# ReLU-squared attention and a PReLU feed-forward layer: quads 5 and 6 turned by transposing transfers, w_out's second half loaded later, FFN2's column halves reordered

## The chip, the cores and the metric

The kernel runs on one core of one Trainium2 chip. The metric is the time of one execution in microseconds (us), as the device reports it; lower is better. TensorE (PE) multiplies matrices, VectorE (DVE), ScalarE (ACT) and GpSimd (POOL) work on elements, SyncE (SP) only issues transfers. Sixteen DMA engines carry the transfers. Those that convert float32 to bfloat16 on the way are issued by POOL, the transposing ones and the stores of the output by SP.

## The reference

Attention with a squared ReLU in place of the softmax, then a feed-forward layer with a leaky ReLU of one slope for each hidden column:

```python
def _attn_ref(q, k, v):                     # (8, 12, 448, 64) each
    S = q.shape[2]
    scale = 1.0 / np.sqrt(q.shape[-1])
    scores = scale * np.matmul(q, k.transpose(0, 1, 3, 2))
    attn = np.maximum(scores, 0.0) ** 2 / S
    return np.matmul(attn, v).astype(np.float32)

def _moe_ref(x, w_in, w_out, alpha):        # w_in (768, 2048), w_out (2048, 768)
    h = x @ w_in
    g = np.maximum(h, 0.0) + alpha * np.minimum(h, 0.0)
    return (g @ w_out).astype(np.float32)
# x is the attention's output as (8 * 448, 768); the result is float32 (3584, 768)
```

## The kernel before

**Units.** Four heads of one batch are a quad; there are 24 quads, three to a batch, numbered through. The 448 positions of a head are split as 64 x 7, so that a quad's q or k is a tile raw of 128 x 2 x 7 x 64, and its v a tile vraw of the same shape. Scores, squares and attention go in seven chunks j to a quad.

**Stages of a quad.** `load_qk` (L97) and `load_v` (L104) bring the three tiles in, 224 KB each in bfloat16, issued by POOL. The matmuls of the scores need q and k with the head dimension on the partitions, tile T. There are two ways to make it. `turn_pe` transposes 28 blocks on TensorE against an identity (L152) into PSUM and copies them out (L155). `turn_dma` has DVE copy q and k into a tile perm (L160), and SP issues one transposing transfer perm to T (L162), 448 KB. Then for each chunk `score_mm` runs four matmuls (L174) into a pair of PSUM banks, `relu` empties the pair on ACT (L183) or DVE (L185, by the letter in a pattern such as "ADAAAAA"), and `square` multiplies the result with itself (L193 on DVE, L191 on ACT). Chunks whose square is still to be done wait in the list `late`; `sq(k)` does the next k. `attnv` runs 28 matmuls (L203) over the squares and v, and writes the quad's part of xT, one half by ACT (L213), one by DVE (L214).

**Feed-forward.** For each batch and each of 16 blocks ff of the hidden columns, `f1` runs six matmuls over xT and w_in (L237), two for each quad of the batch; `f1_out` applies the leaky ReLU with one instruction of ACT (L245) and one of DVE (L246), writes gT, and does one late square. `f2(sb, c, hf)` makes 128 rows (c of 7) and 384 columns (half hf of 2) of the output of two batches: 16 matmuls over gT and w_out (L260), a copy by ACT into one of four buffers osb (L262), two stores by SP (L268). Row chunks c = 0, 1, 2 of batches 0 and 1 need batch 0 alone.

**Order.** It is written out by hand; every engine works through its instructions in this order. PSUM has eight banks, and `take_bank`, `take_pair` and `hold` give out the one that was taken longest ago. Quads 0 to 5 are turned on TensorE, all later ones by transfers. After FFN1 of batch 0 come three groups of FFN2 in column half 0, for c = 0, 1 and 2, with the scores of quads 4 and 5 and attention of quads 3 and 4 between them. FFN1 of batch 1 begins with the matmuls of four blocks over quads 3 and 4, and attention of quad 5 among them. Then the other groups of FFN2 of batches 0 and 1 follow, with the scores of later quads between (`run`, `burst`). Batches 2 to 7 are one loop.

**Queues.** POOL issues all loads in the written order. Three raw buffers each for q and k mean that the load of quad n waits until quad n-3 has been turned. The weights w_out_sb lie in SBUF as two column halves of 1536 KB, one transfer each (L118); w_in_sb is 16 transfers. perm has two buffers, T four, vraw seven.

Of the kernel before, what the change touches and what calls it, by code (L numbers as in the profile page):

```python
# [11 lines left out]
BF16 = mybir.dt.bfloat16  # L12
# [8 lines left out]
def kernel(  # L21
# [10 lines left out]
    nc = tc.nc  # L32
    B, H, S, D = q.shape
# [25 lines left out]
    w_out_sb = singles.tile([128, 2, KF, HALF], BF16)  # L59
    alpha_sb = singles.tile([128, KF], F32)  # L60
    beta_sb = singles.tile([128, KF], F32)
    psum = ps_pool.tile([128, 8, 512], F32)


# [13 lines left out]
    def hold():  # L78

        i = min(range(8), key=lambda i: (taken[i], i))  # L80
        taken[i] = 10**9
        return i

    def take_bank():
        i = min(range(8), key=lambda i: (taken[i], i))
        take(i, 1)
        return psum[:, i]
# [4 lines left out]
    def load_qk(n):  # L92
        b, g = divmod(n, NG)
        for name, src in (("q", q), ("k", k)):
            t = raw_pool.tile([128, 2, NJ, D], BF16, tag=name, name=f"{name}raw")
            flat = src[b].rearrange("(m two) (pp j) d -> (two pp) m (j d)", two=2, j=NJ)
            nc.gpsimd.dma_start(out=t.rearrange("p m j d -> p m (j d)"), in_=flat[:, 2 * g:2 * g + 2])  # L97
            raw[(n, name)] = t

    def load_v(n):  # L100
        b, g = divmod(n, NG)
        t = v_pool.tile([128, 2, NJ, D], BF16, tag="v", name="vraw")
        flat = v[b].rearrange("(m two) (pp j) d -> (two pp) m (j d)", two=2, j=NJ)
        nc.gpsimd.dma_start(out=t.rearrange("p m j d -> p m (j d)"), in_=flat[:, 2 * g:2 * g + 2])  # L104
        vraw[n] = t
# [8 lines left out]
                nc.gpsimd.dma_start(out=w_in_sb[64 * hf:64 * hf + 64, :, e, lo:hi],  # L114
                                    in_=w_in_v[hf, e, :, :, lo:hi])

    def load_w_out(h):
        nc.gpsimd.dma_start(out=w_out_sb[:, h], in_=w_out_v[h])  # L118

    FIRST = 4  # L120
    first, flat0 = {}, {}
# [21 lines left out]
    T = {}  # L143

    def turn_pe(n, parts=(("q", 0, NJ, "D"), ("k", 0, NJ, "D"))):
        if n not in T:
            T[n] = T_pool.tile([128, 2, NJ, 128], BF16, tag="T", name="T")
        for name, lo, hi, eng in parts:
            ps = take_bank().bitcast(BF16)
            for j in range(lo, hi):  # L150
                for s in range(2):
                    nc.tensor.transpose(ps[64 * s:64 * s + 64, 128 * j:128 * j + 128], raw[(n, name)][:, s, j], ident)  # L152
            dst = T[n][:, "qk".index(name), lo:hi].rearrange("p j c -> p (j c)")
            copy = nc.vector.tensor_copy if eng == "D" else nc.scalar.copy
            copy(dst, ps[:, 128 * lo:128 * hi])  # L155

    def turn_dma(n):
        p = perm_pool.tile([128, 2, NJ, 2, D], BF16, tag="perm", name="perm")
        for i, name in enumerate("qk"):
            nc.vector.tensor_copy(p[:, i], raw.pop((n, name)).rearrange("p s j d -> p j s d"))  # L160
        t = T_pool.tile([128, 2, NJ, 128], BF16, tag="T", name="T")
        nc.sync.dma_start_transpose(out=t.rearrange("p a j c -> p (a j) c"),  # L162
                                    in_=p.rearrange("p a j s d -> p (a j s d)"))
        T[n] = t
# [31 lines left out]
    def attnv(n):  # L196
        ps = take_pair()
        vv = vraw.pop(n)
        for j in range(NJ):
            a = att.pop((n, j))  # L200
            for r in range(2):
                for s in range(2):
                    nc.tensor.matmul(ps[64 * s:64 * s + 64, r, :S],  # L203
                                     vv[64 * r:64 * r + 64, s, j, :],
                                     a[64 * r:64 * r + 64, s],
                                     start=(j == 0), stop=(j == NJ - 1))
        b, g = divmod(n, NG)
        if g == 0:
            xT[b] = xT_pool.tile([128, NG, 2, S], BF16, tag="xT", name="xT")
        if n == 0:  # L210
            nc.scalar.activation(xT[b][:, g], ps[:, :, :S], ACTF.Copy, scale=out_scale)
            return
        nc.scalar.activation(xT[b][:, g, 0], ps[:, 0, :S], ACTF.Copy, scale=out_scale)  # L213
        nc.vector.tensor_scalar(xT[b][:, g, 1], ps[:, 1, :S], out_scale, None, ALU.mult)  # L214
# [3 lines left out]
    def sc(chunks):  # L218

        for n, j, eng in chunks:  # L220
            late.append((n, j, relu(score_mm(n, j), eng)))

    def sq(k=99, eng="D"):
        for g in late[:k]:
            square(*g, eng)
        del late[:k]

    def run(chunks):
        sc(chunks)
        sq()  # L230
# [4 lines left out]
    def f1_mm(ps, b, ff, ks):  # L235
        for km in ks:
            nc.tensor.matmul(ps, w_in_sb[:, km // 2, km % 2, bass.ts(ff, 128)],  # L237
                             xT[b][:, km // 2, km % 2, :],
                             start=(km == 0), stop=(km == KM - 1))

    def f1_out(ps, b, ff):
        if b // 2 not in gT:
            gT[b // 2] = g_pool.tile([128, KF, 2 * S], BF16, tag="g", name="gT")
        neg = neg_pool.tile([128, S], F32, tag="neg", name="neg")
        nc.scalar.activation(neg, ps, ACTF.Relu, scale=-1.0)  # L245
        nc.vector.scalar_tensor_tensor(gT[b // 2][:, ff, (b % 2) * S:(b % 2) * S + S],  # L246
                                       neg, beta_sb[:, ff:ff + 1], ps, ALU.mult, ALU.add)
        sq(1)
# [6 lines left out]
    def f2(sb, c, hf, parts=((0, HALF),)):  # L255
        o = o_pool.tile([128, HALF], F32, tag="o", name="osb")
        for lo, hi in parts:
            ps = take_bank()[:, :hi - lo]
            for ff in range(KF):
                nc.tensor.matmul(ps, gT[sb][:, ff, bass.ts(c, 128)], w_out_sb[:, hf, ff, lo:hi],  # L260
                                 start=(ff == 0), stop=(ff == KF - 1))
            nc.scalar.copy(o[:, lo:hi], ps)  # L262
            for u in range(2):
                blk = 2 * c + u
                b, j = 2 * sb + blk // NJ, blk % NJ
                rows = out[b * S:(b + 1) * S].rearrange("(pp j) d -> j pp d", j=NJ)
                eng = nc.scalar if u and hi - lo < HALF else nc.sync
                eng.dma_start(out=rows[j][:, hf * HALF + lo:hf * HALF + hi], in_=o[64 * u:64 * u + 64, lo:hi])  # L268
# [4 lines left out]
    def ch(n, lo, hi, p=pat):  # L273
        return [(n, j, p[j]) for j in range(lo, hi)]
# [22 lines left out]
    sq(1)  # L297
    sc([(1, 4, "D"), (1, 5, "A"), (1, 6, "A")])
    sq(2)
    load_w_out(0)  # L300
    load_v(3)
    early = {}
    todo = []
# [8 lines left out]
    sc(ch(2, 0, 3, "AAA"))  # L312
    sq(3)
    attnv(1)
    load_qk(5)
    load_v(4)
    load_v(5)
    load_w_out(1)
    todo = [(ff, km) for ff in range(4) for km in range(4)]
    sc(ch(2, 3, 5, "AAAAAAA"))  # L320
    sq(2)
# [14 lines left out]
    def f1s(b, lo, hi):  # L336
        for ff in range(lo, hi):
            f1(b, ff)

    def load(n):  # L340
        if n < NQ:
            load_qk(n)
            load_v(n)
# [4 lines left out]
        load(n + 2)  # L348

    turn_pe(3)  # L350
    load_qk(6)
    load_v(6)
    f1s(0, 4, 6)
    sc(ch(3, 0, 3))
    f1s(0, 6, 8)
# [3 lines left out]
    f1_mm(ps, 0, 9, range(KM))  # L359
    turn_pe(4, (("q", 0, NJ, "A"), ("k", 0, NJ, "D")))  # L360
    f1_out(ps, 0, 9)
    load_qk(7)
    load_v(7)
    f1s(0, 10, 12)
    sc(ch(3, 6, 7) + ch(4, 0, 2, "AA"))
    f1s(0, 12, 16)
    f2(0, 0, 0)
    sc(ch(4, 2, 5, "AAADAAA"))
    attnv(3)
    sc(ch(4, 5, 7, "AAAAAAD"))  # L370
    turn_pe(5)
    sq(3)
    sq(2, "A")
    load_qk(8)
    load_v(8)
    f2(0, 1, 0)
    sc(ch(5, 0, 3))
    attnv(4)
    sc(ch(5, 3, 5, "AAAADAA"))
    sq(3)  # L380
    sq(2, "A")
    f2(0, 2, 0)
    sc(ch(5, 5, 7, "AAAAAAD"))
    sq(1, "A")
    sq(1)


    chunks = [(n, j) for n in range(2 * NG, NQ) for j in range(NJ)]
# [2 lines left out]
    def some(k):  # L391
        lo = at_c[0]
        at_c[0] = min(lo + k, len(chunks))
        return [(n, j, e) for (n, j), e in zip(chunks[lo:at_c[0]], "ADA")]

    def burst(n):

        sc(some(3))
        attnv(n)
        sc(some(2))  # L400
        sq()

    early = []
    for ff in range(4):
        ps = take_bank()[:, :S]
        f1_mm(ps, 1, ff, range(4))
        early.append(ps)
        if ff == 1:
            attnv(5)
    for ff in range(KF):  # L410
        if ff < 4:
            f1_mm(early[ff], 1, ff, range(4, KM))
            f1_out(early[ff], 1, ff)
        else:
            f1(1, ff)
        if ff in (1, 4, 7):
            turn_dma(6 + ff // 3)
        if ff == 11:
            load(9)
            load(10)  # L420
    f2(0, 3, 0)
    run(some(3))
    f2(0, 3, 1)
    f2(0, 0, 1)
    prepare(9)
    run(some(3))
    f2(0, 1, 1)
    run(some(3))
    f2(0, 2, 1)
    run(some(3))  # L430
    f2(0, 4, 0)
    burst(6)
    f2(0, 4, 1)
    f2(0, 5, 0)
    prepare(10)
    burst(7)
    f2(0, 5, 1)
    f2(0, 6, 0)
    burst(8)
    f2(0, 6, 1)  # L440

# [56 lines left out]
```

## Time and profile before

| what | us |
|---|---|
| median of 4 runs (388.07 to 388.64) | 388.3 |
| the profiled execution | 387.89 |
| its span, first to last instruction | 386.1 |
| TensorE busy: FFN1 matmuls L237 (768) | 149.8 |
| TensorE busy: FFN2 matmuls L260 (912) | 151.1 |
| TensorE busy: scores L174 (672) | 45.5 |
| TensorE busy: attention L203 (672) | 37.4 |
| DVE busy | 265.9 |
| ACT busy | 206.2 |
| transposing transfers L162 (18), issue to landing, shortest, median, longest | 3.4, 6.9, 13.1 |
| w_out's two halves, issue to landing | 14.5, 22.7 |

Each row of TensorE is the union of that group's instructions. A matmul's own duration is longer than its share, since matmuls are pipelined: one of 384 columns lasts 0.32 us, and 16 of them take 2.6 us together. "Issue to landing" of a transfer includes the time that it spends behind others. The 40 slices of the page are 9.65 us each; the digits are tenths. In the chain that ended last every piece starts when what released it was done, so that the difference between starts is what a piece costs on the way to the end.

### The profile page before, as it was taken

The numbers are of one execution on the slowest core, as the hardware profiler recorded it, in microseconds if no ns is written. First come the engines' busy times: TensorE is split into PE (matmuls) and PEld (weight loads), VectorE is DVE, ScalarE is ACT, GpSimd is POOL, SyncE is SP. The second block draws the span as 40 slices with busy tenths as digits, with TensorE's granted clock in tenths as the row PEclk, the third lists the DMA queues.
The fourth block names the chain that finished last, engine by engine and source line by source line (L and its number), as shares of the span: only waits on it lengthen the run. The fifth ranks groups of instructions, "written<-read, shape, count | busy, mean of one in ns | idle before, by whom it ended". The sixth has DMA issues, their size and how long they took to land.

```text
span 386.1 us, 7917 instructions
## 1 busy us (share of the span) xinstructions
PE 377.7 (98%) x3228; PEld 210.7 (55%) x3228; DVE 265.9 (69%) x421; ACT 206.2 (53%) x332; POOL 64.1 (17%) x95
## 2 busy tenths in 40 slices
PE   7799999999999999999999999999999999999996
PEld 5444564555665456555555455654555545655554
DVE  4987786776868978789655897689754887626300
ACT  5978696446454664465444654547543475434311
POOL 7557221421012202022100221020000000000000
PEclk9999999999999999999999999999999999999999
DMA  9999999999293765687192871936035300120023
GB/s 158 191 201 204 204 213 220 169 181 212 73 164 57 114 129 83 130 131 120 42 182 51 131 121 41 181 55 133 22 74 97 71 0 23 42 61 2 15 70 82
DMA packets 71365, 42.97 MB, mean 111 GB/s; under 512 B 38432, under 2 KB 71328, under 8 KB 71328
## 3 DMA queue, kind: packets, MB, share of 16 engines
q0 software_dynamic: 26768, 22.45, 40.1%
q1 hardware_dynamic: 44128, 19.65, 24.0%
q8 instruction: 25, 0.41, 0.4%
q10 hardware_dynamic: 432, 0.36, 0.3%
q14 instruction: 12, 0.10, 0.1%
HBM read 45.62 MB, written 11.01 MB: 147 GB/s over the span
## 4 chain that ended last, share of the span: by engine, by line
PE 94%; DVE 3%; DMA 1%; ACT 0%; ACTq 0%; issue 0%
PE psum L237 38%; PE psum L260 38%; PE psum L174 9%; PE psum L203 8%; DVE at L193 2%; DMA qfirst<-in_q_dram 1%; PE psum L152 1%; DVE T L155 1%; DVE rl L185 1%; ACT osb L262 0%; ACTq L268 0%; ACT T L155 0%; DVE qraw L136 0%; ACTq L262 0%
## 5 line engine op out<-in xcount | busy, mean ns | idle before, releaser
L260 PE MATMUL psum<-w_out_sb,gT 128*128 128x384 bf16 (+2 forms) x912 | 151.1, 323 | 0.0
L237 PE MATMUL psum<-xT,w_in_sb 128*128 128x448 bf16 x768 | 149.8, 353 | 0.0
L260 PEld LDWEIGHTS <-gT 128*128 128x128 bf16 x912 | 86.7, 98 | 63.0 <-issue 8.2
L237 PEld LDWEIGHTS <-w_in_sb 128*128 128x128 bf16 x768 | 73.6, 98 | 72.3 <-issue 5.7
L246 DVE SCALAR_TENSOR_TENSOR gT<-neg,beta_sb,psum 128x448 bf16<-128x448 f32 x128 | 83.2, 677 | 29.8 <-ACT neg L245 29.8
L245 ACT ACTIVATE neg<-psum 128x448 f32<-128x448 f32 x128 | 69.2, 546 | 63.3 <-PE psum L237 59.6
L183 ACT ACTIVATE rl<-psum 128x896 bf16<-128x896 f32 x112 | 97.3, 935 | 0.5 <-PE psum L174 0.5
L193 DVE TENSOR_TENSOR at<-rl 128x896 bf16<-128x896 bf16 x162 | 90.7, 618 | 0.0
L185 DVE TENSOR_SCALAR rl<-psum 128x896 bf16<-128x896 f32 x56 | 60.8, 1087 | 43.1 <-PE psum L174 43.1
L262 ACT COPY osb<-psum 128x384 f32<-128x384 f32 (+2 forms) x57 | 27.0, 473 | 105.3 <-PE psum L260 98.5
L174 PE MATMUL psum<-T 64*64 64x448 bf16 x672 | 45.5, 356 | 2.8 <-DVE T L155 1.0
L97 POOL DMA_DIRECT2D qraw<-in_q_dram x23 | 16.6, 720 | 168.7 <-DVE perm L160 161.0
L203 PE MATMUL psum<-at,vraw 64*64 64x448 bf16 x672 | 37.4, 351 | 0.3 <-DVE at L193 0.2
L203 PEld LDWEIGHTS <-vraw 64*64 64x64 bf16 x672 | 24.1, 106 | 10.8 <-issue 2.9
L174 PEld LDWEIGHTS <-T 64*64 64x64 bf16 x672 | 18.2, 105 | 21.4 <-issue 14.4
L214 DVE TENSOR_SCALAR xT<-psum 128x448 bf16<-128x448 f32 x23 | 14.4, 625 | 16.3 <-PE psum L203 11.9
L97 POOL DMA_DIRECT2D kraw<-in_k_dram x23 | 16.6, 722 | 15.7 <-DMA w_out_sb<-in_moe_w_out_dram 14.2
L104 POOL DMA_DIRECT2D vraw<-in_v_dram x24 | 17.5, 729 | 1.8 <-DMA qraw<-in_q_dram 0.7
L213 ACT ACTIVATE xT<-psum 128x448 bf16<-128x448 f32 x23 | 12.6, 550 | 3.3 <-PE psum L203 3.3
L160 DVE COPY perm<-qraw 128x896 bf16<-128x896 bf16 x18 | 11.0, 613 | 2.5 <-DMA T<-perm 2.5
L114 POOL DMA_DIRECT2D w_in_sb<-in_moe_w_in_dram x16 | 10.1, 630 | 7.4 <-DMA kraw<-in_k_dram 2.3
L160 DVE COPY perm<-kraw 128x896 bf16<-128x896 bf16 x18 | 11.0, 609 | 0.0
(24 smaller groups left out, 40.8 us busy)
## 6 DMA issues: line engine op xcount, KB each, us to landing
out_dram<-osb SPq DMA_DIRECT2D x110, 96.0 KB, 2.2
vraw<-in_v_dram POOLq DMA_DIRECT2D x24, 224.0 KB, 7.9
qraw<-in_q_dram POOLq DMA_DIRECT2D x23, 224.0 KB, 4.9
kraw<-in_k_dram POOLq DMA_DIRECT2D x23, 224.0 KB, 6.7
w_in_sb<-in_moe_w_in_dram POOLq DMA_DIRECT2D x16, 192.0 KB, 8.4
w_out_sb<-in_moe_w_out_dram POOLq DMA_DIRECT2D x2, 1536.0 KB, 18.6
qfirst<-in_q_dram SPq DMA_DIRECT2D x1, 448.0 KB, 4.2
T<-perm SPq DMA_TRANSPOSE x18, 6.9
```

The source lines that it names most:

```text
L97: nc.gpsimd.dma_start(out=t.rearrange("p m j d -> p m (j d)"), in_=flat[:, 2 * g:2 * g + 2])
L160: nc.vector.tensor_copy(p[:, i], raw.pop((n, name)).rearrange("p s j d -> p j s d"))
L174: nc.tensor.matmul(ps[64 * c:64 * c + 64, r, :S], t[64 * r:64 * r + 64, 1, j, 64 * c:64 * c + 64], t[64 * r:64 * r + 64, 0, :, 64 * c:64 * ...
L183: nc.scalar.activation(rl, ps[:, :, :S], ACTF.Relu)
L185: nc.vector.tensor_scalar(rl, ps[:, :, :S], 0.0, None, ALU.max)
L193: nc.vector.tensor_tensor(a, rl, rl, ALU.mult)
L203: nc.tensor.matmul(ps[64 * s:64 * s + 64, r, :S], vv[64 * r:64 * r + 64, s, j, :], a[64 * r:64 * r + 64, s], start=(j == 0), stop=(j == NJ ...
L237: nc.tensor.matmul(ps, w_in_sb[:, km // 2, km % 2, bass.ts(ff, 128)], xT[b][:, km // 2, km % 2, :], start=(km == 0), stop=(km == KM - 1))
L245: nc.scalar.activation(neg, ps, ACTF.Relu, scale=-1.0)
L246: nc.vector.scalar_tensor_tensor(gT[b // 2][:, ff, (b % 2) * S:(b % 2) * S + S], neg, beta_sb[:, ff:ff + 1], ps, ALU.mult, ALU.add)
L260: nc.tensor.matmul(ps, gT[sb][:, ff, bass.ts(c, 128)], w_out_sb[:, hf, ff, lo:hi], start=(ff == 0), stop=(ff == KF - 1))
L262: nc.scalar.copy(o[:, lo:hi], ps)
```

## The change

Quad 5 is turned by a transposing transfer in place of TensorE, right after FFN1 of batch 0, and quad 6 after the scores of quad 4 in place of FFN1 of batch 1. The loads of q and k of quad 5 are issued ahead of w_out's first half, which comes in four transfers of four blocks ff each. GpSimd copies one element of quad 5's T into a new tile `landed` between the loads of quad 6's q and k and those of quads 7 and 8, and w_out's second half, also in four transfers, is issued behind the loads of quads 9 and 10 during FFN1 of batch 1. The square of chunk (4, 1) is kept back behind quad 5's turn. Groups 1 and 2 of FFN2 now lie next to each other; the scores of quad 5 follow them, the last two chunks among the early FFN1 matmuls of batch 1, which now are five blocks in held banks. FFN2 does all groups of column half 0 before those of half 1.

```diff
--- before.py
+++ after.py
@@ -59,6 +59,7 @@
     w_out_sb = singles.tile([128, 2, KF, HALF], BF16)
     alpha_sb = singles.tile([128, KF], F32)
     beta_sb = singles.tile([128, KF], F32)
+    landed = singles.tile([1, 1], BF16)
     psum = ps_pool.tile([128, 8, 512], F32)
 
 
@@ -114,8 +115,9 @@
                 nc.gpsimd.dma_start(out=w_in_sb[64 * hf:64 * hf + 64, :, e, lo:hi],
                                     in_=w_in_v[hf, e, :, :, lo:hi])
 
-    def load_w_out(h):
-        nc.gpsimd.dma_start(out=w_out_sb[:, h], in_=w_out_v[h])
+    def load_w_out(h, step=KF):
+        for lo in range(0, KF, step):
+            nc.gpsimd.dma_start(out=w_out_sb[:, h, lo:lo + step], in_=w_out_v[h][:, lo:lo + step])
 
     FIRST = 4
     first, flat0 = {}, {}
@@ -297,7 +299,8 @@
     sq(1)
     sc([(1, 4, "D"), (1, 5, "A"), (1, 6, "A")])
     sq(2)
-    load_w_out(0)
+    load_qk(5)
+    load_w_out(0, 4)
     load_v(3)
     early = {}
     todo = []
@@ -312,10 +315,8 @@
     sc(ch(2, 0, 3, "AAA"))
     sq(3)
     attnv(1)
-    load_qk(5)
     load_v(4)
     load_v(5)
-    load_w_out(1)
     todo = [(ff, km) for ff in range(4) for km in range(4)]
     sc(ch(2, 3, 5, "AAAAAAA"))
     sq(2)
@@ -348,8 +349,6 @@
         load(n + 2)
 
     turn_pe(3)
-    load_qk(6)
-    load_v(6)
     f1s(0, 4, 6)
     sc(ch(3, 0, 3))
     f1s(0, 6, 8)
@@ -359,30 +358,37 @@
     f1_mm(ps, 0, 9, range(KM))
     turn_pe(4, (("q", 0, NJ, "A"), ("k", 0, NJ, "D")))
     f1_out(ps, 0, 9)
-    load_qk(7)
-    load_v(7)
     f1s(0, 10, 12)
     sc(ch(3, 6, 7) + ch(4, 0, 2, "AA"))
-    f1s(0, 12, 16)
+    f1s(0, 12, 14)
+    kept = late[:]
+    del late[:]
+    f1s(0, 14, 16)
+    turn_dma(5)
+    late += kept
+    load_qk(6)
+    nc.gpsimd.tensor_copy(landed, T[5][:1, 0, 0, :1])
+    load_qk(7)
+    load_qk(8)
+    load_v(6)
+    load_v(7)
+    load_v(8)
     f2(0, 0, 0)
+    sq()
     sc(ch(4, 2, 5, "AAADAAA"))
     attnv(3)
     sc(ch(4, 5, 7, "AAAAAAD"))
-    turn_pe(5)
     sq(3)
     sq(2, "A")
-    load_qk(8)
-    load_v(8)
+    sq()
+    turn_dma(6)
     f2(0, 1, 0)
+    f2(0, 2, 0)
     sc(ch(5, 0, 3))
+    sq(1)
     attnv(4)
     sc(ch(5, 3, 5, "AAAADAA"))
-    sq(3)
-    sq(2, "A")
-    f2(0, 2, 0)
-    sc(ch(5, 5, 7, "AAAAAAD"))
-    sq(1, "A")
-    sq(1)
+    sq()
 
 
     chunks = [(n, j) for n in range(2 * NG, NQ) for j in range(NJ)]
@@ -401,41 +407,46 @@
         sq()
 
     early = []
-    for ff in range(4):
-        ps = take_bank()[:, :S]
-        f1_mm(ps, 1, ff, range(4))
-        early.append(ps)
+    for ff in range(5):
+        early.append(hold())
+        f1_mm(psum[:, early[ff], :S], 1, ff, range(4))
         if ff == 1:
+            sc(ch(5, 5, 7))
+            sq(1)
+            sq(1, "A")
+        if ff == 3:
             attnv(5)
     for ff in range(KF):
-        if ff < 4:
-            f1_mm(early[ff], 1, ff, range(4, KM))
-            f1_out(early[ff], 1, ff)
+        if ff < 5:
+            f1_mm(psum[:, early[ff], :S], 1, ff, range(4, KM))
+            f1_out(psum[:, early[ff], :S], 1, ff)
+            take(early[ff], 1)
         else:
             f1(1, ff)
-        if ff in (1, 4, 7):
-            turn_dma(6 + ff // 3)
-        if ff == 11:
+        if ff in (1, 4):
+            turn_dma(7 + ff // 3)
+        if ff == 6:
             load(9)
             load(10)
+            load_w_out(1, 4)
     f2(0, 3, 0)
     run(some(3))
-    f2(0, 3, 1)
-    f2(0, 0, 1)
+    f2(0, 4, 0)
+    f2(0, 5, 0)
     prepare(9)
     run(some(3))
+    f2(0, 6, 0)
+    run(some(3))
+    f2(0, 0, 1)
+    run(some(3))
     f2(0, 1, 1)
-    run(some(3))
+    burst(6)
     f2(0, 2, 1)
-    run(some(3))
-    f2(0, 4, 0)
-    burst(6)
-    f2(0, 4, 1)
-    f2(0, 5, 0)
+    f2(0, 3, 1)
     prepare(10)
     burst(7)
+    f2(0, 4, 1)
     f2(0, 5, 1)
-    f2(0, 6, 0)
     burst(8)
     f2(0, 6, 1)
```

## The prediction

> Times are us from the start of the profiled span. "T5" is quad 5's tile T, q5, k5, v5 its three loads, f2(c,h) FFN2's group of row chunk c and column half h of batches 0 and 1.
>
> **What bounds the kernel.** I read the busy table and the 40 slices first, then the waits of TensorE, then the chain that ended last in order of time from 44 on, then the transfers with their landings.
>
> ```profile
> PE 377.7 (98%) x3228; PEld 210.7 (55%) x3228; DVE 265.9 (69%) x421; ACT 206.2 (53%) x332; POOL 64.1 (17%) x95
> ...
> PEclk9999999999999999999999999999999999999999
> DMA  9999999999293765687192871936035300120023
> ```
>
> TensorE is the bound, at an undiminished clock. Its waits add up to 4.8 and all lie before 20. The DMA engines are full for ten slices, to about 96, and nearly idle late: what the change moves among the transfers lies in the full part, where a late transfer can take the place of the work removed. The chain there is TensorE without a hole, columns start, duration, work:
>
> ```profile
> 45.27 2.60 PE psum L260 x16
> 47.87 0.69 PE psum L174 x12
> 48.56 1.39 PE psum L203 x28
> 49.95 0.38 PE psum L174 x8
> 50.33 0.90 PE psum L152 x28
> 51.24 2.71 PE psum L260 x16
> 53.94 0.69 PE psum L174 x12
> 54.63 1.39 PE psum L203 x28
> 56.03 0.38 PE psum L174 x8
> 56.41 2.71 PE psum L260 x16
> 59.11 0.50 PE psum L174 x8
> 59.61 1.62 PE psum L237 x8
> 61.23 1.45 PE psum L203 x28
> 62.68 16.75 PE psum L237 x88
> ```
>
> The reader is to see the 0.90 at 50.33: quad 5's 28 transposes, the only work that the change takes from TensorE. Quad 6 is turned by a transfer already. The row of those transfers, then POOL waiting for a landing:
>
> ```profile
> T<-perm SPq DMA_TRANSPOSE x18, 6.9
> ...
> DMA to landing us min/median/max: 3.4/6.9/13.1
> ```
>
> ```profile
> 44.93 0.71 POOL L97 DMA_DIRECT2D kraw<-in_k_dram  x1 [7.01 <-DMA w_out_sb<-in_moe_w_out_dram]
> ```
>
> **TensorE's new order, summed.** From 45.27 with the durations above: f2(0,0) 2.60; 12 score matmuls 0.69; attnv(3) 1.39; 8 score matmuls 0.38; f2(1,0) 2.71 and f2(2,0) 2.60 (a group after another FFN2 group costs 2.60: two together are 5.31 in the chain at 82.73), to 55.64; 12 scores 0.69; attnv(4) 1.39; 8 scores 0.38; 8 early FFN1 matmuls 1.62; 8 scores 0.50; 8 early 1.62; attnv(5) 1.45, to 63.29; then the other 80 FFN1 matmuls. These last: 16.75 less eight at 0.19 (96 take 18.16 late in the chain, 8 take 1.62, so 0.188 each and 0.12 for a block's start), 15.25, to 78.54. Before it was 79.44. Saved: **0.90**. Two block starts decide its bounds: joining f2(1,0) to f2(2,0) saves 0.11, splitting the early FFN1 matmuls once more costs 0.12. Without the one 0.78, without the other 1.01. After 78.54 the columns change their order only; the sequence of FFN2 groups, score runs and bursts has the same lengths, so nothing is added.
>
> **DVE and ACT.** Two copies out of PSUM (0.62 each) go, two perm copies (0.61 each) come: even. The stretch from 55.64 to 63.29 now has no FFN2 group between quad 5's scores. By the spacing of consecutive rows (ACT: relu 0.80, square 0.87, xT 0.44, osb 0.37; DVE: relu 1.00, square 0.54, xT 0.54) ACT has 5.7 of work in these 7.65 and DVE 5.8. The tightest points: the square of chunk 6 on ACT ends at about 62.6, attnv(5) reads it at 61.84 + 6/7 x 1.45 = 63.08; the second half of xT leaves DVE at 64.07 (0.15 after attnv's end as at 62.83, then 0.63) and FFN1 reads it four early matmuls and one more later, at 64.35. PSUM banks, followed through the rotation, are free at each step. I cost this at nothing; the cover is 0.3 to 0.5. The 1-element GpSimd copy costs DVE nothing that a row shows; it blocks POOL's queue, see below.
>
> **q5 and k5 ahead of w_out's first half.** Loads land in order. k4 landed at 36.7 (issued 29.16, 7.5 to landing), the first half at 44.4 (29.88 + 14.5): 7.7 for 1536 KB. Five 224 KB loads then took 44.4 to 50.05, 1.13 each. Now q5 and k5 go first, to 38.95, and the quarters land at 40.9, 42.8, 44.7 and 46.65. f2(0,0) reads the last quarter after 12 of 16 matmuls, at 47.22: margin 0.57, cost nothing. From above: the second half took 8.5 (50.05 to 58.56, beside output stores); at that pace the last quarter lands at 47.45 and costs 0.24. A gain is excluded: f2(0,0) waits for nothing now. v3 lands at 47.8 for attnv(3) at 48.56. v4 and v5 keep their 50.05, since the same set lies before them.
>
> **T5.** On DVE the gT rows of ff 14 and 15 start at 45.66 and 46.79 with a square of 0.54 between; the change holds that square back, so ff 15 starts at 46.25, the perm copies at 46.84 and 47.38, done at 47.99. SP issued the first transfer 0.08 after its copies (67.62 to 67.70), so 48.07. POOL's queue has v4 to k6 in flight, as k8, v8 and the next loads were at 67.70; that transfer took 6.9. T5 lands at 54.94, scores need it at **55.64**: no stall, margin 0.70. From both sides: alone it was 3.4; the longest with no transposing transfer ahead were 8.06 (issued at 107.78 and 150.84, behind two output stores on the same queue), which here means 56.13 and a stall of 0.5. I take 6.9, the row with the same company. The stores of f2(0,0) stand behind T5 on SP; four osb buffers cover them, and without that cover only ACT's copy of a later group waits.
> The Trainium skill (VectorE: DVE Perf Modes, The three transpose paths and Rules for kernel authors) speaks against this step: transpose 128x128 on TensorE if a PSUM destination will do, with 390 ns there against 1309 ns by DMA. By it quad 5's 14 blocks would take an estimated 18.3 by DMA, T5 would land at 66.4, and the kernel would lose about 9.9. The trace does not bear out that price: all 14 blocks of a quad landed in 3.4 to 13.1.
>
> **q6 and k6, T6.** Without T5 k6 would land at 50.05 + 2 x 1.13 = 52.3. Beside a transfer the second load landed together with it (132.56: T at 139.35, k at 139.30; 165.57: 172.45 and 172.48), so k6 at about 55. DVE reaches T6's copies at 53.2, waits there, and is done at 55.6; queued behind is the relu of (5,1), ready at 56.1, and behind it the pair of banks that chunk (5,4) takes at 57.9. Some 0.5 are spare; if T5 is late, this is late with it. T6 itself is first read at 81.1 and would land at 62.8.
>
> **w_out's second half.** POOL now waits for T5 (about 55) before q7 to v8 (seven loads, 0.72 each to issue); q9, k9, v9 follow; q10 waits until T7's copies free its buffer (about 67.5); then come k10, v10 and the quarters. First need: f2(0,1) at 78.54 + 2.60 + 0.69 + 5.31 + 0.69 + 2.71 + 0.69 = 91.23, its last quarter at 93.3. Landing: q7 at 55.1 + 4.4 (3.9 and 4.8 from the rows at 105.58 and 67.40) = 59.5; 12 loads 13.6; the half 7.7; then T6, T7, T8. What a transfer takes from the loads: from 69.70 to 95.35 twelve loads landed, 13.6 of 25.65; six stores of 96 KB at 200 GB/s are 2.9; T6 to T8 and most of a fourth transfer share the other 9.1, 2.4 each, or 4.0 if the stores and the fourth cost nothing. So 59.5 + 13.6 + 7.7 + 7.2 + 2.0 (four stores) = 90.0, or 92.8 with 4.0 and no stores. With 8.5 for the half and T9 (issued at about 88) beside its end, 95. I take 90, cost nothing. The loads behind it, 11 and 12, are due only in batch 2.
> The skill (Advanced Engine Details and Errata, X-Bar Transpose) has transposing transfers as fast as regular ones, 350 to 400 GB/s; T's 448 KB would then be an estimated 1.2 each and the half would land some 3.6 earlier. No such transfer landed within less than 3.4 here.
>
> **Sum.** The profiled execution took 387.89 (span 386.1, 1.8 around it). Less 0.90: 386.99, span 385.2. The median of the runs is 388.3, 0.41 above that execution: 387.4.
>
> **Rivals.**
> (a) *T5 or k6 late.* The wait moves to the scores of quad 5, or to DVE at T6's copies. For: margin 0.7 and 0.5, rows of 8.06. Against: those rows had stores ahead. Price 0.2 to 0.7: 387.9.
> (b) *f2(0,0) waits for the last quarter*, or attnv(3) for v3. For: margin 0.57 on an estimated landing. Against: the pace of 1.13 and 7.7 is steady up to 50. Price 0.2 to 0.6: 387.8.
> (c) *Slower: w_out's second half late at f2(0,1).* Place: its last quarter at 93.3. For: every load from q7 on stands behind T5, the engines are full to 96 already, and three transfers lie among them. Against: loads 11 and 12 no longer precede it, about 6.8 of the 95.35. At a landing of 93.3 it begins to cost, at 94.2 the gain is gone, from 95.0 it is slower by over 0.2%. With 95.3 the wait is 2.0: 389.4.
> That the transposes stay in another form can be excluded: only L152 makes them.
>
> **How the numbers follow.** 0.2% is 0.78, about what a measurement tells from no change; my forecast of 0.90 lies just beyond. Forecast 0.52 (faster 0.44, same 0.08, as its own range is 387.1 to 387.6); (a) 0.16 (0.04, 0.09, slower 0.03); (b) 0.10 (0.02, 0.07, 0.01); (c) 0.22 (0, 0.04, 0.18). Together faster 0.50, same 0.28, slower 0.22. The range goes from 386.9 (saving 1.01 and scatter of the runs) to 389.4 ((c)'s price).
>
> **What would show it.** Right: L152 with 140 matmuls; T5 landing before 55.6; no wait of TensorE after 45; FFN1 of batch 1 ending about 0.9 earlier than 79.4. Wrong: a wait of L174 on T's transfer or on DVE near 56, of L260 on w_out near 47 or near 91 to 95; or a DVE row at L160 held beyond 56.

## The result and the profile after

The changed kernel takes 387.67 us (median of 42 runs, 387.17 to 388.36), the kernel before 388.26 (60 runs): a ratio of 0.9985, 95% interval 0.9981 to 0.9989. That is 0.59 us less, or 0.15%, with an interval that leaves out no change; it is two thirds of the 0.90 that was forecast, and below the 0.78 (0.2%) that the prediction took for what a measurement just tells from no change. The stated range of 386.9 to 389.4 holds the time.

The busy table and the slices of the changed kernel:

```profile
PE 377.7 (98%) x3200; PEld 211.1 (55%) x3200; DVE 266.3 (69%) x422; ACT 205.4 (53%) x331; POOL 67.8 (18%) x102
...
PEclk9999999999999999999999999999999999999999
DMA  9999999999993666598292772946036300120023
```

TensorE has 28 instructions less, the clock is whole, and the DMA engines are now full for twelve slices in place of ten. The chain that ended last, in order of time, over the stretch that the prediction summed:

```profile
45.86 2.60 PE psum L262 x16
48.46 0.69 PE psum L176 x12
49.15 1.39 PE psum L205 x28
50.55 0.38 PE psum L176 x8
50.93 5.31 PE psum L262 x32
56.23 0.69 PE psum L176 x12
56.92 1.39 PE psum L205 x28
58.31 0.38 PE psum L176 x8
58.69 1.62 PE psum L239 x8
60.31 0.50 PE psum L176 x8
60.81 1.62 PE psum L239 x8
62.43 1.45 PE psum L205 x28
63.88 15.24 PE psum L239 x80
```

The row of the transposes is gone, two FFN2 groups are one piece of 5.31, and no wait has come in. FFN1 of batch 1 ends at 79.12; from the first FFN2 group that is 33.26, where it was 34.17: 0.91 saved. But everything here is 0.59 later than forecast, and the span is 386.0 against 386.1. Two other stretches must have given the gain back. The first is the start. The first FFN1 matmuls in the chain, before and after:

```profile
20.21 0.91 PE psum L237 x4
```

```profile
20.80 0.92 PE psum L239 x4
```

The difference is made between 5 and 8 us, around quad 0's turn. The second is the end. ACT's last two copies of output, timeline of ACT, kernel before and then the changed one (start, duration, and in brackets the idle time before):

```profile
381.72 0.37 ACT L262 COPY osb<-psum 128x256 f32<-128x256 f32 x1 [1.27 <-PE psum L260]
...
382.72 0.27 ACT L262 COPY osb<-psum 128x128 f32<-128x128 f32 x1 [0.62 <-PE psum L260]
```

```profile
381.69 0.37 ACT L264 COPY osb<-psum 128x256 f32<-128x256 f32 x1 [1.55 <-PE psum L262]
...
382.68 0.27 ACT L264 COPY osb<-psum 128x128 f32<-128x128 f32 x1 [0.63 <-PE psum L262]
```

The changed kernel's last matmul starts at 382.00, before it was 382.32, 0.32 earlier; the copy starts only 0.03 to 0.04 earlier. Measured from the start of the last matmul of its own group (381.37 and 381.05), the first of the two copies starts after 0.35 before and after 0.63 in the changed kernel; the second waits for ACT's own store in between and is late with it. The chain has the same place as follows, before and then in the changed kernel. ACTq is the end of ACT's wait for TensorE, and "issue" is time in which ACT waited for nothing that the profile shows:

```profile
381.66 0.03 ACTq L262
381.68 0.04 issue
381.72 0.38 ACT osb L262
```

```profile
381.34 0.03 ACTq L264
381.37 0.32 issue
381.69 0.38 ACT osb L264
```

ACT had TensorE's signal 0.32 earlier and began only 0.04 earlier: 0.28 is lost at the very end, behind TensorE.

### The profile page after: what moved, and what is told of

The parts are those of the page before. It is cut to its first block, busy times and chain, and to the rows that moved or that the text cites. A ratio compares the mean times of both kernels' runs of the same rounds, so it can differ in the third digit from the quotient of the medians.

```text
span 386.0 us, 7874 instructions
## 1 busy us (share of the span) xinstructions
PE 377.7 (98%) x3200; PEld 211.1 (55%) x3200; DVE 266.3 (69%) x422; ACT 205.4 (53%) x331; POOL 67.8 (18%) x102
## 4 chain that ended last, share of the span: by engine, by line
PE 94%; DVE 3%; DMA 1%; issue 0%; ACT 0%; ACTq 0%
PE psum L239 38%; PE psum L262 38%; PE psum L176 9%; PE psum L205 8%; DVE at L195 2%; DMA qfirst<-in_q_dram 1%; PE psum L154 1%; DVE T L157 1%; DVE rl L187 1%; ACT osb L264 0%; ACTq L270 0%; DVE qraw L138 0%; ACTq L264 0%
## 5 line engine op out<-in xcount | busy, mean ns | idle before, releaser
L195 DVE TENSOR_TENSOR at<-rl 128x896 bf16<-128x896 bf16 x164 | 91.8, 618 | 0.0
L187 DVE TENSOR_SCALAR rl<-psum 128x896 bf16<-128x896 f32 x55 | 59.8, 1086 | 43.6 <-PE psum L176 43.6
```

Source lines behind the costliest of these rows:

```text
L187: nc.vector.tensor_scalar(rl, ps[:, :, :S], 0.0, None, ALU.max)
L195: nc.vector.tensor_tensor(a, rl, rl, ALU.mult)
```

## The experiments

### Where the missing 0.3 is: the start

The new tile `landed` is allocated in SBUF ahead of the first loads' tiles and moves all that follow. Three kernels ask whether that costs the 0.3: the changed one with the tile behind all others, the kernel before with an unused tile, and the changed one with quad 5 turned on TensorE again.

```diff
 # landed_last: a pool of its own behind the others
-    landed = singles.tile([1, 1], BF16)
+    landed = landed_pool.tile([1, 1], BF16)
 # landed_only: the kernel before
+    landed = singles.tile([1, 1], BF16)
```

> The changed kernel with the tile landed taken from a pool behind all others, so that no other tile moves in SBUF (in the changed kernel landed takes 32 bytes ahead of the first tiles, raw and all that follow). Theory S, the moved addresses cost about 0.3 us in the first 12 us: 387.35 us, first FFN1 matmul at about 20.2 as before. Theory N, the 0.3 that are missing from the predicted 0.90 are lost elsewhere: 387.67 us as the changed kernel, first FFN1 matmul anywhere from 20.2 to 20.8.

> The kernel before with the tile landed allocated at the changed kernel's place and never used, so that the same tiles move by 32 bytes and nothing else changes. Theory S: 388.55 us, 0.3 slower than before, first FFN1 matmul at about 20.8. Theory N: 388.26 us, no difference.

landed_last: 387.39 us (11 runs), ratio 0.9978, 0.9970 to 0.9987; first FFN1 matmul at 20.32. landed_only: 388.23, ratio 1.0004, 0.9996 to 1.0013; first FFN1 matmul at 20.51. Neither time alone tells S from N. The first interval holds 387.35 and 387.67, and the second holds no change and the 0.3 of S (1.0008); but landed_only's fastest run, 387.85, is that of the kernel before beside it, 387.86, where S wants 0.3 more. The profiles decide: two kernels below that keep the moved tiles (pe5, act_minus1) start FFN1 at 20.21, as the kernel before, and act_minus1 profiled a second time starts it at 20.59. So theory S falls. The start differs from one execution to the next (20.2 to 20.8 over the profiles) and goes with none of the edits; what makes it differ is open.

```diff
 # pe5: the changed kernel
-    turn_dma(5)
     late += kept
-    nc.gpsimd.tensor_copy(landed, T[5][:1, 0, 0, :1])
     sc(ch(4, 5, 7, "AAAAAAD"))
+    turn_pe(5)
     sq(3)
```

> The changed kernel with quad 5 turned on TensorE again, where it was turned before, and without GpSimd's copy; the tile landed keeps its place, everything else stays moved. Both theories: 0.90 us more than the changed kernel, 388.55 us, 28 transposes of 0.90 in the chain. If the other moves hide a gain or a loss of their own, it is not 0.90: 388.26 would say that they cost 0.3.

pe5: 388.24 us, ratio 1.0005, 0.9996 to 1.0014. By the medians that is 0.57 more than the changed kernel, not 0.90. The chain of pe5 says 0.90 all the same:

```profile
45.27 2.60 PE psum L262 x16
...
50.33 0.90 PE psum L154 x28
51.23 5.31 PE psum L262 x32
...
79.43 2.60 PE psum L262 x16
```

From 45.27 to 79.43 is 34.16, the kernel before to 0.01. From there to the start of TensorE's last matmul it is 302.88 in pe5, in the kernel before and in the changed one. So the moved loads, the other order of the column halves and the merged groups together neither gain nor lose anything on TensorE; the whole gain is the 28 transposes. In pe5 the first of the last two copies starts 0.65 after its last matmul, like in the changed kernel: the late end came with the edits around, not with the turn. Its fastest run, 388.10, is 0.93 above the changed kernel's 387.17; the ratios are 0.20% or 0.78 us apart, and their intervals are too wide to tell 0.57 from 0.90.

### Where the missing 0.3 is: the end

Counted over all of ACT's records in the trace, semaphore waits included, the late copy is number 576 in every kernel in which it is late, and 575 in those in which it is not (the expectations count one more). The change made the program one longer, 584 records in place of 583; the page shows one less (331 against 332), since it leaves the waits for semaphores out. Two kernels move the copy by one, by giving the square of chunk (5, 6) to the other engine.

```diff
 # act_minus1: the changed kernel
-            sq(1)
-            sq(1, "A")
+            sq(2)
 # before_act_plus1: the kernel before
-    sq(1, "A")
-    sq(1)
+    sq(2, "A")
```

> The changed kernel with the square of chunk (5, 6) on DVE in place of ACT, so that ACT's program has one instruction less and the first of the last two osb copies is its 576th and not its 577th. Theory T, that instruction begins 0.28 us late because of its position in ACT's program: the copy follows the last matmul's start by 0.35 us as before, and the time is 387.4 us. Rival R, the late copy belongs to the moved loads or to the stores: 0.63 us and 387.67 us stay.

> The kernel before with the square of chunk (5, 6) on ACT in place of DVE, so that ACT's program has one instruction more. Theory T: the first of the last two osb copies follows its last matmul's start by 0.63 us in place of 0.35, and the time is 388.5 us, 0.28 more than before. Rival R: 0.35 us and 388.26 us.

Timelines of ACT, act_minus1 and then before_act_plus1:

```profile
380.82 0.37 ACT L264 COPY osb<-psum 128x256 f32<-128x256 f32 x1 [1.27 <-PE psum L262]
```

```profile
382.45 0.37 ACT L262 COPY osb<-psum 128x256 f32<-128x256 f32 x1 [1.56 <-PE psum L260]
```

The idle time of 1.27 comes back with one instruction less, that of 1.55 with one more; from the last matmul it is 0.35 and 0.65. act_minus1 took 386.9 us (7 runs), ratio 0.9975, 0.9965 to 0.9985; before_act_plus1 388.56, ratio 1.0008, 0.9999 to 1.0016, an interval that just holds no change, so that here the timeline decides and not the time. Both went the way of theory T; R falls, since the late copy comes in the kernel before without any moved load. The eight kernels of this study with the late copy have it at number 576, and the four without at 575. What happens there is open: whether the position counts or the length of the whole program was not told apart, and in the gap of the changed kernel (381.3 to 381.8) the trace has no packet but those of the output's stores, so no transfer of the program either.

> The same kernel as act_minus1, timed beside the changed kernel on one chip. Theory T, the 0.28 us at the end are the whole of what is missing from the predicted 0.90: about 0.9 less than before, 387.2 to 387.3 us, and 0.28 less than the changed kernel. If the first timing was luck: as the changed kernel.

> The changed kernel once more, as the reference beside act_minus1_again: about 0.6 less than before.

Side by side on one chip: act_minus1 387.01 (10 runs), ratio 0.9976, 0.9967 to 0.9985; the changed kernel 387.70 (11 runs), ratio 0.9989, 0.9980 to 0.9998. The medians are 0.69 apart, more than 0.28; the ratios are 0.13% or 0.5 us apart with intervals that reach 0.28, and the fastest runs, 386.88 and 387.18, are 0.30 apart. The version with the square on DVE beats both kernels and has the forecast gain, 0.24%.

### What keeps quad 5's T in time

The prediction gave T5 a landing of 6.9 us after its issue. These four kernels take away or weaken what the change does for it.

```diff
 # no_gate_no_tile: the changed kernel
-    landed = singles.tile([1, 1], BF16)
-    nc.gpsimd.tensor_copy(landed, T[5][:1, 0, 0, :1])
 # gate_behind7: the changed kernel
-    nc.gpsimd.tensor_copy(landed, T[5][:1, 0, 0, :1])
     load_qk(7)
+    nc.gpsimd.tensor_copy(landed, T[5][:1, 0, 0, :1])
 # wout_early: the changed kernel
     load_v(4)
     load_v(5)
+    load_w_out(1, 4)
 ...
     load(10)
-    load_w_out(1, 4)
 # dma5_only: the kernel before
     sc(ch(4, 5, 7, "AAAAAAD"))
-    turn_pe(5)
+    turn_dma(5)
```

> The changed kernel without GpSimd's copy and without the tile landed: the loads of quads 7 and 8 no longer wait for quad 5's T. Theory S: 387.35 us if T5 still lands before 56; theory N: 387.67 us. If the copy is what brings T5 in time, T5 lands 1.5 or more later than its 54.1, the scores of quad 5 wait 0.5 to 1.5 at about 56, and the time is that much longer under either theory.

> The changed kernel with GpSimd's copy behind the loads of q7 and k7 in place of ahead of them. Theory D, the transposing transfer is delayed by each load queued ahead of or beside it: without the copy T5 took 15.2 us in place of 5.4 beside eight more loads, 1.2 for each; two loads make it land at 56.5 to 57, the scores wait 0.3 to 0.8 us, 388.0 to 388.5 us. Rival, it is starved only once POOL has filled its queue of eight: T5 stays at 54.1, 387.67 us.

> The changed kernel with w_out's second half, still in quarters, issued behind v5 as before the change. Theory D, a transposing transfer gets its turn when the loads queued beside it have landed: the half keeps the queue full 7.7 us longer, to about 60, T5 lands at 62 to 63 in place of 54.1, the scores wait 6 to 7 us at 56.2, 394 us. Rival, the prediction's view (6.9 us beside any traffic): T5 at about 55.5, no wait, 387.7 us, and moving the half was not needed.

> The kernel before with quad 5 turned by a transfer at the place of its transposes and nothing else changed. Issued at about 52.8 into a queue that stays full to 70. Prediction's view, 6.9 us: T5 at 59.7, needed at 53.0, a wait of 6.7 and 394 us. Theory D, 15 us as without the copy: T5 at 68, a wait of 15 and about 402 us.

| kernel | T5 issued | T5 landed | took | scores wait | median us | ratio, 95% interval |
|---|---|---|---|---|---|---|
| changed | 48.67 | 54.09 | 5.4 | 0 | 387.67 | 0.9985, 0.9981 to 0.9989 |
| gate_behind7 | 48.47 | 56.68 | 8.2 | 0.7 | 388.35 | 1.0027, 1.0001 to 1.0053 |
| wout_early | 48.47 | 62.55 | 14.1 | 6.2 | 396.45 | 1.0222, 1.0208 to 1.0236 |
| no_gate_no_tile | 48.06 | 63.24 | 15.2 | 7.7 | 397.90 | 1.0249, 1.0234 to 1.0264 |
| dma5_only | 53.32 | 68.31 | 15.0 | 14.8 | 404.30 | 1.0421, 1.0407 to 1.0436 |

The waits of TensorE, no_gate_no_tile and then wout_early (what waited, for what, total, times, longest):

```profile
PE psum L175 <- DMA T<-perm: 7.7, 1, 7.7
```

```profile
PE psum L176 <- DMA T<-perm: 6.2, 1, 6.2
```

Theory D has the direction right in all four: the landing goes with how long the load queue stays full after the issue. T5 does not have to wait until that queue is empty, though: in no_gate_no_tile it landed at 63.24, and loads issued beside it landed until 67.85. The sizes were missed in part. no_gate_no_tile was expected to wait 0.5 to 1.5 and waited 7.7, and wout_early and dma5_only took some 2.4 us more than the expected 394 and 402 (the last section has what comes on top of a wait). Two of the 11 runs of gate_behind7 took 392.6 and 393.0, the others 387.8 to 388.7; the two were not profiled.

The transfers of no_gate_no_tile from 53 to 61, while T5 was under way beside loads (queue, packets, MB, time of the packets as a share of the 16 engines):

```profile
q0 software_dynamic: 1404, 1.19, 90.6%
q1 hardware_dynamic: 1407, 0.36, 33.3%
```

The loads' queue and that of the transposing transfer moved the same number of packets, to 3 in 1400, and a packet of a load is three to four times as large. T5 has 1792 packets of 256 bytes. At 176 a microsecond they take 10.2, and before the first one some 4 pass when the queue is full at the issue (52.05 against 48.06 here): 14 to 15 together. In the changed kernel they had the engines to themselves from 52.4 on:

```profile
q1 hardware_dynamic: 1161, 0.34, 129.3%
```

That is the window from 52.4 to 53.5, some 1000 packets a microsecond. The loads of q6 and k6, issued before T5 on POOL's queue, landed at 51.19 and 52.31, where the prediction had them without T5 (51.2 and 52.3).

The Trainium skill (DMA: Bandwidth & Descriptors, Queues, rings and completion order) says that each DMA engine takes turns between the queues it has work for, packet by packet. The 1404 against 1407 packets, as the profile counts them, fit that.

### The price of a late second half of w_out

```diff
 # wout_behind11: the changed kernel
             load(10)
-            load_w_out(1, 4)
 ...
     prepare(9)
+    load_w_out(1, 4)
```

> The changed kernel with w_out's second half issued behind the loads of quad 11. The prediction's price for a late half: three loads of 1.13 us and the transposing transfers among them bring the last quarter from 91.2 to 95 to 96, TensorE reads it at about 93.8 and waits 1 to 2 us, 388.7 to 389.9 us. Rival, the margin is larger than it looks because the DMA engines have room there: no wait, 387.67 us.

390.85 us, ratio 1.0072, 1.0043 to 1.0101, single runs from 388.3 to 393.9: above the expected 388.7 to 389.9. The profiled execution took 393.88, one of the longest, so its wait is longer than most. In it the last quarter landed at 98.17, and TensorE waited

```profile
PE psum L262 <- DMA w_out_sb<-in_moe_w_out_dram: 4.4, 2, 3.8
```

Three loads more ahead of the half cost 7 us of its landing there (91.18 in the changed kernel), not 3.4 and some. They cost it at the issue: POOL issues the last quarter at 79.75 in place of 72.19, and from there it takes 18.4 in place of 19.0. The margin in the changed kernel is real, 2.7 (93.84 to 91.18), and by 7 us for three loads little more than one would use it up (an estimate).

## Why the prediction was right, and where not

**The gain on TensorE** was right in place and size: 0.90 forecast, 0.91 in the profile, with the sequence of pieces as summed; pe5 shows that nothing else contributes. (By its own terms the bounds beside it are 0.79 and 1.02, not 0.78 and 1.01.)

**"After 78.54 ... nothing is added"** is the step that failed. TensorE's part of it holds, but the sum took TensorE's end for the kernel's end. With one instruction more in ACT's program the first of the last two output copies came 0.28 late, and 0.91 - 0.28 = 0.63 is about what the medians show, 0.59. So the forecast of 0.90, just beyond 0.2%, became a measured 0.59, just within it.

**T5 at 6.9 us, "the row with the same company"**, gave the right outcome, no stall, for a wrong reason: 5.4 measured. The company was not the same. The transfer issued at 67.70 had three loads in flight and five more issued within 4 us behind it, and from 72.2 to 73.0 no packet of a load was under way; T5 had four in flight and none behind. With a queue that stays full it is 14 to 15, outside the stated bounds of 3.4 to 8.06, so that the margin held by luck as far as the prediction's own reason goes. GpSimd's copy was costed as something that only blocks POOL's queue; it and the moved half of w_out each hold back loads that would delay T5, and without either the kernel is 2.2% to 2.5% slower than before. The prediction named no price for that cover being gone. k6 was put at 55 for the same reason and landed at 52.31.

**w_out's quarters.** First half: 46.65 forecast, 46.67 measured, with no wait. Second half: 90.0 forecast, which is 90.6 with this execution's start, and 91.18 measured; within its bounds, no wait. **DVE and ACT** made TensorE wait nowhere in the dense stretch, as costed.

**Rivals.** (a) and (c) did not happen, but both mechanisms exist where the experiments provoke them, at a higher price than stated: 7.7 us of waiting for T5 where (a) had 0.7, and 4.4 for the half, in one of the longest executions, where (c) had 2.0. (b) did not happen. T7 and T8 took 15.4 and 19.6 in the changed kernel, unseen, since the first scores that read them come 8 and 5 us later.

## What to carry to other kernels

A transposing transfer that is needed soon was cheap here only where the load queue beside it ran dry (5.4 us against 14 to 15): hold the loads back until it has landed, and put large loads that nobody needs yet behind it. When a change is worth less than a microsecond, follow the sum past the bounding engine to the last store, and look at the end in the profile of more than one kernel. Kernels that differ by one instruction elsewhere can tell a lost fraction at the end from the change itself.

## What the runs showed of the hardware that was not expected

ACT's last copy but one begins 0.28 us late in the eight kernels in which it is number 576 of ACT's records, and in none of the four in which it is number 575, with nothing in the profile that it waits for.

In the wait of 7.7 us TensorE's granted clock was halved, and it stayed so for some us behind it. Windows of no_gate_no_tile (stretch, length, busy times and counts, granted clock, DMA share, GB/s):

```profile
55.00:63.00 8.00, 0.63 (x4) 0.17 (x2) 0.00 (x0) 0.48 (x1) 1.22 (x2) 0.74 1.24 199
63.00:68.00 5.00, 4.71 (x49) 2.14 (x50) 2.25 (x3) 2.46 (x4) 0.00 (x0) 0.50 1.28 177
68.00:72.00 4.00, 4.00 (x24) 1.59 (x24) 3.73 (x6) 2.08 (x3) 0.00 (x0) 0.87 0.42 128
72.00:80.00 8.00, 8.00 (x64) 4.17 (x63) 5.19 (x10) 5.40 (x11) 2.34 (x4) 1.00 0.11 3
```

From 63 to 68, just after T5 landed, it was 0.50, and whole again from 72 on: the same pieces take longer (attention's matmuls 2.61 in place of 1.39), so that the long waits here cost some 2 to 3 us more than they lasted (the time grew by 10.2 with the wait of 7.7, by 8.8 with that of 6.2).
